# T chain on VectorE and ScalarE alone, last layer in two passes, attention steps in a written-out order

## Chip, cores and metric

One core of one Trainium2 chip. The metric is device time of one launch in microseconds (us). Engines in the text: TensorE (PE, with its weight loads PEld), VectorE (DVE), ScalarE (ACT), GpSimd (POOL) and SyncE (SP), which issues the DMAs.

## What is computed

Three layers in a row, on 3072 tokens (4 batches of 768) of width 384 (8 heads of 48). All of it is float32; `w_in` and `w_out` of the last layer arrive as float64 bits.

```python
# 1. linear attention with a complex decay, one state per head
mag = sqrt(a_re*a_re + a_im*a_im); scale = minimum(mag, 0.999) / (mag + 1e-6)
for t in range(768):                       # a = (a_re + i a_im) * scale
    S = a[t] * S + k[t] v[t]^T             # complex state 48 x 48, k and v real
    y[t] = q[t] @ real(S)
# 2. soft mixture of 8 experts with 4 slots each
logits = x @ phi
d = softmax over tokens; slot_input = d.T @ x
slot_out = relu(slot_input @ w1[e]) @ w2[e]
c = softmax over slots;  x = c @ slot_out
# 3. last layer, d_ff = 2048
h = maximum(x @ w_in, 0); out = (h * h) @ w_out
```

## The kernel before, in words

**Attention** works in 24 units of 128 tokens (6 per batch). The decay is taken in the log domain: for every chunk of up to three units (9 chunks, `TUS`), the **T chain** (`plan_t`, from L797) turns `a_re` and `a_im`, laid out as 128 x 3w with w = 128 to 384, into running sums of log magnitude (`t3`) and of angle (`t4`). Its steps in order: a clamp (L822, DVE), Ln and Exp (ACT), the ratio a_im / a_re by a multiply on GpSimd (L825), a clamp (L826, DVE), its square, Ln and a second square with a sum for a range flag (ACT), two combining steps (L830, L832, DVE) with an Exp between them, a running sum (three scans, L835, DVE), Arctan (ACT), again three scans, and a wrap into one turn (L842 to an integer, L845, DVE). `spans` and `waves` transpose the sums by unit (L881) and make from them E (exponentials) and W (cosine and sine).

Each unit (`plan_u`, from L935) multiplies q and k by E (`decay`, L964) and by W (`rotate`, L970) on DVE, transposes them on PE (`flip`, L988), copies them out of PSUM (`flop`, on ACT or DVE), makes four-head score blocks (`sc`, L1036), masks them on DVE (L1040), adds the unit's part to the state (`kv`, L1013; `keepS` keeps it), and forms y (`y1`, L1051 and L1056), which is copied (`ye`), transposed (`yb`, L1072) and copied again (`ya`). Every four units `grp_steps` adds to the token softmax; at the end `merge_steps` closes it.

**Order.** Every step is entered with `Plan.add` (engine, cost, due time, what it needs, buffers it takes and gives back). `Plan.issue` walks a modelled clock: whenever a modelled engine is free, it emits the ready step with the earliest due time, shifted by a table `SHIFT`. Where PE has nothing to do in the model, `warm` emits pairs of idle matmuls (L1169). The result is a fixed instruction stream per engine, executed in order on the chip. The 16 blocks of `w_in` are decoded from float64 among these steps (`plan_wi`, L1110; `f64_steps`: one ACT step and four DVE steps, L459 to L472). Weights of the experts are 16 loads of 1.5 MB (L491), three without a condition, six behind the end of the T chain and of the rotations (`l1` to `l3`), the rest when the attention's buffers are gone.

**After the steps** `grp_flags` (L493 to L503) makes the range flags on DVE and one matmul, the experts follow (`finish`: `up`, `turn`, `down`), and four of the 16 blocks of `w_out` are decoded beside them (`weights_out`).

**Last layer** (from L646): `seq` is 6 groups of 512 tokens by 16 blocks f of 128 hidden columns. Step n does on PE `up_last(n+2)` (one matmul, L680) and nine matmuls into three PSUM banks (`sh` times the high and the low part of w_out, `sl` times the high part, L729 and L726); ACT makes s and sh from the `up` result, DVE makes q (ACT for n = 1 to 11) and `sl` (GpSimd for n = 1 to 15, L697). In the first group each step also folds one `w_in` block with the experts' output (`make_G`, L668) and decodes one `w_out` block (`weights_out`). A group's three banks are copied out and stored after f = 15.

Of the kernel before, what the change touches and what calls it, by code (L numbers as in the profile page):

```python
# [11 lines left out]
F32 = mybir.dt.float32  # L12
# [12 lines left out]
NU = B * NCH  # L25
# [11 lines left out]
C_ID, C_CAUS, C_SEL, C_HM, C_BE, C_BO = 0, 128, 256, 544, 568, 600  # L37
C_W = 728
AR_MIN, AR_MAX, X_LIM, L_MIN = 1e-5, 1e18, 1.56, -65.0
R_MAX, X4_MAX, E_MIN = 2500.0, 5.9, 1e-26  # L40
# [3 lines left out]
SHIFT = {  # L44
# [3 lines left out]
    "across": -167.5, "back": -81.0, "bank": 277.5, "cos": -145.8, "decay": 8.4, "ends": 10.9, "exps": -7.8,  # L48
    "flip00": 13.5, "flip01": 17.2, "flip10": 8.4, "flip11": 1.7, "flop00": 0.5, "flop01": -7.4, "flop10": 0.4,
    "flop11": 9.4, "gather": 34.8, "keep": -203.0, "keepS": -7.6, "keep_c": 39.8, "keep_d": 387.9, "keep_l":  # L50
    -20.0, "keep_s": -201.7, "kv": -40.8, "l1": -34.8, "l2": 203.6, "l3": 305.6, "ld_a": -142.8, "ld_a1": 63.5,
    "ld_q": -102.8, "ld_raw": -133.3, "ld_v": 109.8, "less": 161.1, "logits": 12.6, "mask0": -50.2, "mask1": -1.2,
    "masked": -3.6, "over": -346.4, "pre": 127.7, "rot0": -69.6, "rot1": 7.7, "sc0": 9.7, "sc1": -8.7, "scale":
    -2.9, "share": 103.1, "size": 16.1, "slots": 137.4, "spread": 19.3, "sums": 331.4, "t3": -214.8, "t4": -274.4,
    "top": -22.5, "top_m": 39.4, "total": -24.9, "turn_d": -240.0, "turn_l": -54.1, "weight": -43.9, "wi0": -0.5,
    "wi1": 24.5, "wi2": 39.3, "wi3": -2.9, "wi4": 17.8, "y10": -57.3, "y11": 6.6, "y12": -65.0, "y13": -141.5,
    "ya": -1.5, "yb": 43.0, "ye": 5.7
}
WI_0, WI_P = 50.0, 10.909090909090908
# [7 lines left out]
def const_array():  # L67
# [12 lines left out]
    c[:, C_BO:C_BO + 128] = (p[:, None] % NS == p[None, :] % NS)  # L80
# [3 lines left out]
class Plan:  # L84
# [4 lines left out]

    LAG, LOAD, HOLD, KEEP, T_WARM, SECOND = 0.2, 1.28, 31.3, 0.43, 10.0, 325.2  # L90
# [4 lines left out]
    def add(self, eng, cost, due, fn, after=(), get=(), put=(), lat=0.0, tab=None, key=None):  # L95

        engs = [eng] if eng in ("PE", "SP") else list(eng)
        key = key or fn.__name__
        due += SHIFT.get(key, 0.0) + SHIFT.get(self.group, 0.0)
        self.steps.append((dict(zip(engs, cost if len(engs) > 1 else [cost])), due, fn,  # L100
                           [a for a in after if a is not None], get, put, lat, tab))
        return len(self.steps) - 1

    def issue(self, warm):
# [3 lines left out]
        ready = {"SP": [], "D": [], "A": [], "G": [], "PE": []}  # L108

        def enter(i):  # L110
            for e in self.steps[i][0]:
                ready[e].append(i)
        for i, s in enumerate(self.steps):
            for a in s[3]:
                users[a].append(i)
            if not missing[i]:
                enter(i)
        events, busy = [], {}
        now, done = 0.0, 0
        left = sum("PE" in s[0] for s in self.steps)  # L120

        def other(i):
            return self.steps[i][7] not in (None, self.loaded[0])

        def fits(i):
            get = self.steps[i][4]
            return all(self.free[g] >= get.count(g) for g in get)

        def due(i, eng):
            return self.steps[i][1] + self.HOLD * other(i) + self.SECOND * (eng == "D" and "A" in self.steps[i][0])  # L130
        while done < n:
            for eng, todo in ready.items():
                if busy.get(eng, 0) > now:
                    continue
                _, i = min(((due(i, eng), i) for i in todo if fits(i)), default=(0, None))
                if i is not None:
                    costs, _, fn, _, get, _, lat, _ = self.steps[i]
                    for e in costs:
                        ready[e].remove(i)
                    for g in get:  # L140
                        self.free[g] -= 1
                    left -= eng == "PE"
                    busy[eng] = end = now + costs[eng] + self.LOAD * other(i)
# [3 lines left out]
                elif eng == "PE" and left and events and now >= self.T_WARM and warm():  # L147
# [4 lines left out]
            while events and events[0][0] <= now + 1e-9:  # L152
                _, over, i = heapq.heappop(events)
                if over:
# [3 lines left out]
                    for j in users[i]:  # L158
                        missing[j] -= 1
                        if not missing[j]:  # L160
                            enter(j)
# [91 lines left out]
def moe_kernel(ctx, tc, raw, cst, aT, qk, vv_d, phi, w1, w2, w_in, w_out, out):  # L253
# [16 lines left out]
    lim = const.tile([128, 2], F32, name="lim")  # L270
# [22 lines left out]
    def grp_steps(g, st, p_s, ps_m):  # L293
# [64 lines left out]
        return [("PE", 1.18, logits, dict(needs="y", get=["pt"], put=["y"] * 4)),  # L358
                ("AD", (0.2, 0.25), keep_l, dict(put=["pt"])),
                ("D", 0.55, top, dict()),  # L360
                ("A", 0.5, exps, dict(tab=SET_EXP)),
                ("D", 0.1, total, dict(side=1)),
                ("PE", 0.11, turn_l, dict(get=["pt"])),
                ("AD", (0.16, 0.2), keep_c, dict(put=["pt"])),
                ("PE", 0.11, turn_d, dict(get=["pt"])),
                ("AD", (0.16, 0.2), keep_d, dict(put=["pt"])),
                ("PE", 0.75, sums, dict(needs="x", get=["pt"], put=["x"] * 4)),
# [880 lines left out]
```

## Time and profile before

| | |
|---|---|
| median of 3 runs | 576.48 us (575.58 to 578.71) |
| profiled execution | 572.69 us, of which the span is 570.9 us |
| PE busy in the span | 94% |
| DVE, ACT, POOL busy | 80%, 66%, 8% |
| attention: first to last instruction ahead of the experts | 0 to 288.35 us |
| experts | 288.35 to 316.42 us |
| last layer, until the last matmul | 316.42 to 564 us |

The profiled execution's own time is 3.8 us under the median. Busy shares are means over three stages with different limits, so the rows below are taken by stage. A row of a window gives the busy time of each engine in it; a row of a line gives count, busy time, mean of one, and the idle time in front with what ended it.

### The profile page before, as it was taken

Reading aid. Unit: us, or ns where it says so; the run is one execution under the profiler, and the core shown is the slowest. Engines: PE = TensorE matmul, PEld = TensorE weight load, DVE = VectorE, ACT = ScalarE, POOL = GpSimd, SP = SyncE. Lnnn points to the kernel's source line nnn. Section 1 sums busy time; section 2 is a strip of 40 time slices with the busy share of each in tenths; the row PEclk is TensorE's granted clock in tenths of the full one; section 3 lists DMA queues with packets and bytes.
Section 4 is the critical chain, followed back from the end, with each engine's and each line's share of the span. In section 5 each row is a group of like instructions: output and inputs, shape, how many; then the busy total and the mean of one; then the engine's idle time right before and its main releaser. Section 6 shows DMA issues by size and latency. Waiting matters only on the chain.

```text
span 570.9 us, 10386 instructions
## 1 busy us (share of the span) xinstructions
PE 534.1 (94%) x4080; PEld 430.2 (75%) x4080; DVE 454.4 (80%) x740; ACT 375.1 (66%) x684; POOL 45.2 (8%) x28
## 2 busy tenths in 40 slices
PE   1989999999998989999999997799999999999995
PEld 1977787878787878787843886588878888788884
DVE  3989999999999999998647799966666666666552
ACT  5887889888898868783213678555555555555551
POOL 1011020012001020000000133310000000000000
PEclk9999999999999989999999999799999999999999
DMA  8762342433415223398996133010010100100101
GB/s 304 295 259 87 111 124 85 151 115 111 125 44 171 67 65 116 122 386 311 396 389 254 55 112 103 10 56 1 0 57 0 57 0 0 56 2 0 56 1 61
DMA packets 23961, 67.25 MB, mean 118 GB/s; under 512 B 2144, under 2 KB 12256, under 8 KB 21856
## 3 DMA queue, kind: packets, MB, share of 16 engines
q1 hardware_dynamic: 23904, 66.51, 33.6%
q8 instruction: 34, 0.56, 0.4%
q14 instruction: 23, 0.19, 0.1%
HBM read 61.78 MB, written 4.72 MB: 116 GB/s over the span
## 4 chain that ended last, share of the span: by engine, by line
PE 61%; DVE 16%; ACT 1%; issue 1%; POOL 0%; DVEq 0%; POOLq 0%; ACTq 0%
PE po L729 20%; PE po L726 11%; PE pt L1036 4%; PE pt L988 4%; PE ph L680 3%; PE py L1051 3%; DVE t L835 2%; PE pt L527 2%; PE pS L1013 2%; PE py L1056 2%; DVE dw L472 2%; PE pt L1169 2%; DVE qke L964 1%; PE pt L542 1%; DVE dx L459 1%; DVE dx L469 1%
## 5 line engine op out<-in xcount | busy, mean ns | idle before, releaser
L729 PE MATMUL po<-sh,woh 128*128 128x512 f32 x288 | 114.5, 398 | 3.0 <-ACT sh L276 3.0
L729 PE MATMUL po<-sh,wol 128*128 128x512 f32 x288 | 114.2, 397 | 0.0
L276 ACT ACTIVATE s<-ph 128x512 f32<-128x512 f32 x96 | 57.2, 595 | 75.3 <-PE ph L680 72.9
L687 DVE TENSOR_TENSOR q<-s 128x512 f32<-128x512 f32 x85 | 60.6, 713 | 53.4 <-ACT s L276 53.3
L726 PE MATMUL po<-sl,woh 128*128 128x512 f32 x288 | 86.7, 403 | 1.2 <-POOL sl L697 1.2
L729 PEld LDWEIGHTS po<-sh,woh 128*128 128x128 f32 x288 | 54.6, 189 | 16.6 <-ACT sh L276 3.7
L726 PEld LDWEIGHTS po<-sl,woh 128*128 128x128 f32 x288 | 54.7, 192 | 16.0 <-POOL sl L697 3.3
L729 PEld LDWEIGHTS po<-sh,wol 128*128 128x128 f32 x288 | 54.6, 190 | 12.7
L697 DVE TENSOR_TENSOR sl<-q,sh 128x512 fp32r<-128x512 f32 x81 | 56.0, 692 | 9.6
L276 ACT ACTIVATE sh<-s 128x512 fp32r<-128x512 f32 x96 | 60.7, 633 | 3.5
L276 ACT ACTIVATE T<-pt 96x512 f32<-96x512 f32 x81 | 45.3, 593 | 17.9 <-PE pt L988 17.4
L1036 PE MATMUL pt<-T,T 96*128 96x128 f32 x384 | 52.0, 281 | 0.0
L1169 PE MATMUL pt<-cs 128*128 128x128 f32 x284 | 40.2, 291 | 12.0 <-DMA cs<-in_const_dram 11.8
L1036 PEld LDWEIGHTS pt<-T,T 96*128 96x128 f32 x384 | 46.2, 192 | 3.5 <-issue 3.0
L1169 PEld LDWEIGHTS pt<-cs 128*128 128x128 f32 x284 | 36.4, 202 | 14.2 <-DMA cs<-in_const_dram 11.8
L1051 PE MATMUL py<-am,v 128*48 128x128 f32 x384 | 40.9, 291 | 2.5 <-DVE am L1040 2.5
L680 PE MATMUL ph<-cT,G 128*128 128x512 f32 x96 | 39.8, 415 | 0.1
L825 POOL TENSOR_TENSOR a<-a,t 128x1152 f32<-128x1152 f32 (+2 forms) x9 | 24.3, 2702 | 180.6 <-ACT t L291 164.5
L835 DVE TENSOR_TENSOR_SCAN t<-a,lim 128x384 f32<-128x384 f32 (+2 forms) x39 | 36.7, 994 | 0.2 <-ACT a L291 0.2
L1040 DVE TENSOR_TENSOR am<-pt,cs 128x512 f32<-128x512 f32 x48 | 32.6, 682 | 4.3 <-PE pt L1036 3.7
L697 POOL TENSOR_TENSOR sl<-q,sh 128x512 fp32r<-128x512 f32 x15 | 20.7, 1384 | 147.6 <-PE ph L680 119.6
L1056 PE MATMUL py<-T,S 96*48 96x128 f32 x320 | 31.6, 275 | 0.0
(155 smaller groups left out, 931.9 us busy)
## 6 DMA issues: line engine op xcount, KB each, us to landing
w<-in_w_dram SPq DMA_DIRECT2D x16, 1536.0 KB, 9.3
qk<-in_qk_dram SPq DMA_DIRECT2D x24, 384.0 KB, 3.2
a<-in_a_dram SPq DMA_DIRECT2D x14, 576.0 KB, 4.2
raw<-in_wi_dram SPq DMA_DIRECT2D x16, 384.0 KB, 4.7
raw<-in_wo_dram SPq DMA_DIRECT2D x16, 384.0 KB, 3.1
v<-in_vn_dram SPq DMA_DIRECT2D x24, 192.0 KB, 2.4
out_dram<-o SPq DMA_DIRECT2D x18, 256.0 KB, 2.5
a<-in_a_dram SPq DMA_DIRECT2D x2, 384.0 KB, 6.1
```

The costliest lines, as they stand in the source:

```text
L276: return nc.scalar.activation(*args, **kw)
L680: mm(p, G[:, 128 * f:128 * (f + 1)], R["cT", g], start=True, stop=True)
L687: V.tensor_tensor(out=q, in0=s, in1=s, op=ALU.mult)
L697: (nc.gpsimd if 0 < n < 16 else V).tensor_tensor(out=sl, in0=s, in1=sh, op=ALU.subtract)
L726: mm(po[c], R["woh"][:, f, 128 * c:128 * (c + 1)], sl, start=False, stop=f == 15)
L729: mm(po[c], R[w][:, f, 128 * c:128 * (c + 1)], sh, start=f == 0 and w == "woh", stop=False)
L835: V.tensor_tensor_scan(out=v3(out)[:, j], data0=v3(src)[:, j], data1=low.to_broadcast([128, w]), initial=first[:, j:j + 1] if first is not ...
L1036: mm(p[:, C * h:C * (h + 1)], st["T", u, 1, g][:, h], st["T", u, 0, g][:, h], start=True, stop=True)
L1040: V.tensor_tensor(out=m, in0=st["pa", u, g].rearrange("p (h t) -> p h t", h=4), in1=cs[:, C_CAUS:C_CAUS + C].unsqueeze(1).to_broadcast([12 ...
L1051: mm(p[64 * w:64 * w + D, C * pr:C * (pr + 1)], st["v", u][:, h], st["am", u, h // 4][:, h % 4], start=True, stop=fst)
L1056: mm(p[64 * w:64 * w + D, C * pr:C * (pr + 1)], st["S", u][:, h], st["T", u, 0, h // 4][:, h % 4], start=False, stop=True)
L1169: mm(p[:, :C], ident, ident, start=True, stop=True)
```

## The change

1. **T chain.** Both clamps go (L822, L826), so does GpSimd: the ratio is a DVE multiply. The square and the flag's reduction are one DVE instruction (`tensor_tensor_reduce`, accumulating the maximum); both ACT squares go. The subtraction of L832 moves into the scan, whose second operand is now a full tensor in place of a broadcast limit; a one-operand minimum stays of L832. The conversion to an integer (L842) moves from DVE to ACT.
2. **Last layer.** `seq` goes through f = 0 to 7 for all six groups, then f = 8 to 15 for all six. Only 8 blocks of `w_in` are decoded in the attention; 8 of `w_in` and 8 of `w_out` are decoded beside the first pass, 2.4 pieces a step. The first pass copies its three banks to SBUF (two on ACT, one on DVE), the second adds them on DVE and stores. All `sl` and nearly all q are on DVE. PSUM: four banks for `up`, four for the sums.
3. **Order.** `SHIFT` and the due times no longer decide; `ORDER` lists all 1093 steps by engine, and `issue` takes each engine's list in that order. Costs in the plan are set anew.
4. Small: the merge's broadcast sum (`over`) is four matmuls of 32 rows.

In `ORDER`, the steps that may go on either engine are written into the list of one: 13 of the 96 `flop` copies, 3 `ye`, 4 `ya` and 2 first-unit `keepS` are in DVE's list. ACT's list changes its table 22 times. DVE's list ends with the last copy of the merge (`keep_s`), then two steps of the eighth `w_in` block, a memset and its last two steps.

```diff
-            step("D", D2, lambda: V.tensor_scalar(out=g("a0"), in0=g("a0"), scalar1=AR_MIN, scalar2=AR_MAX, op0=ALU.max, op1=ALU.min))
             step("A", A1, lambda: tact(SET_EXP, g("a0"), g("a0"), AF.Ln), tab=SET_EXP)
-            step("G", P1, lambda: nc.gpsimd.tensor_tensor(out=g("a1"), in0=g("a1"), in1=g("t2"), op=ALU.mult))
-            step("D", D2, lambda: V.tensor_scalar(out=g("a1"), in0=g("a1"), scalar1=X_LIM, scalar2=-X_LIM, op0=ALU.min, op1=ALU.max))
-            step("A", A1, lambda: act(g("t2"), g("a1"), AF.Square), key=("sq", v))
-            step("A", A1 + 0.09, lambda: act(g("t2"), g("t2"), AF.Square, accum_out=flags[:, 1, v:v + 1]), side=1, put=["t2"], key=("x4", v))
+            step("D", D1, lambda: V.tensor_tensor(out=g("a1"), in0=g("a1"), in1=g("t2"), op=ALU.mult), needs=("a1", v))
+            step("D", D1, lambda: V.tensor_tensor_reduce(
+                out=g("t2"), in0=g("a1"), in1=g("a1"), scale=1.0, scalar=0.0, op0=ALU.mult, op1=ALU.max,
+                accum_out=flags[:, 1, v:v + 1]), key=("sq", v))
-            step("D", D1, lambda: V.scalar_tensor_tensor(out=g("a0"), in0=g("a0"), scalar=LN_CLIP, in1=g("t3"), op0=ALU.min, op1=ALU.subtract))
+            step("D", D2, lambda: V.tensor_scalar(out=g("a0"), in0=g("a0"), scalar1=LN_CLIP, scalar2=None, op0=ALU.min))
-            step("D", D3, lambda: sums(g("t3"), g("a0"), ALU.max, lim[:, :1], None), put=["a0"], key=("L", v))
+            step("D", D3, lambda: sums(g("t3"), g("a0"), ALU.subtract, lambda j: v3(g("t3"))[:, j], None), put=["a0"], key=("L", v))
-            step("D", D2, lambda: V.tensor_scalar(out=g("a1").bitcast(I32), in0=g("t4"), scalar1=1.0 / (2 * math.pi), scalar2=None, op0=ALU.mult))
+            step("A", A1, lambda: act(g("a1").bitcast(I32), g("t4"), AF.Copy, scale=1.0 / (2 * math.pi)))
...
-                _, i = min(((due(i, eng), i) for i in todo if fits(i)), default=(0, None))
+                i = line[0]
+                if not missing[i] and all(self.free[g] >= get.count(g) for g in get):
+                    line.popleft()
...
-        for n in range(16):
+        for n in range(HALF):
             plan_wi(n)
...
+        jobs = [(1, f) for f in range(HALF)] + [(o, f) for f in range(HALF, 16) for o in (0, 1)]
...
+            seq = [(g, f) for fs in (range(HALF), range(HALF, 16)) for g in range(6) for f in fs]
+            def beside_last():
+                yield from pieces(R.pop("parts"))
+                for m in range(HALF, len(jobs), 2):
+                    yield from pieces(decode(m))
+                    steps = decode(m + 1)
+                    yield from pieces(steps[:3])
+                    make_G(jobs[m][1])
+                    yield from pieces(steps[3:])
+            rest, paced = beside_last(), [0]
...
-                if not 0 < n < 12:
+                if not 0 < n < 8:
                     V.tensor_tensor(out=q, in0=s, in1=s, op=ALU.mult)
-                (nc.gpsimd if 0 < n < 16 else V).tensor_tensor(out=sl, in0=s, in1=sh, op=ALU.subtract)
+                V.tensor_tensor(out=sl, in0=s, in1=sh, op=ALU.subtract)
...
+                if n < HALF:
+                    if f + 5 < HALF:
+                        make_G(f + 5)
+                    if f + 4 < HALF:
+                        weights_out(f + 4)
+                while paced[0] < (n - 3) * PACE and next(rest, True) is None:
+                    paced[0] += 1
...
+                        if f < HALF:
+                            o[g, c] = p_o.tile([128, 512], F32, name=f"o{g}{c}")
+                            copy("D" if c == 1 else "A", o[g, c], po[c])
+                        else:
+                            V.tensor_tensor(out=o[g, c], in0=po[c], in1=o[g, c], op=ALU.add)
+                            nc.sync.dma_start(out=out[128 * c:128 * (c + 1), 512 * g:512 * (g + 1)], in_=o[g, c])
```

## Rows read from the trace of the kernel before

**Rows 1.** The page: engine, busy us (share of span) and instructions; chain by engine.
```profile
PE 534.1 (94%) x4080; PEld 430.2 (75%) x4080; DVE 454.4 (80%) x740; ACT 375.1 (66%) x684; POOL 45.2 (8%) x28
PE 61%; DVE 16%; ACT 1%; issue 1%; POOL 0%; DVEq 0%; POOLq 0%; ACTq 0%
```

**Rows 2.** Windows: length, busy us of PE, PEld, DVE, ACT, POOL; clock, DMA share, GB/s.
```profile
0.00:288.35 288.35, 264.89 (x2644) 223.25 (x2647) 261.55 (x428) 222.19 (x407) 24.53 (x13) 0.99 0.51 174
...
40.00:250.00 210.00, 201.74 (x2056) 168.33 (x2056) 204.27 (x305) 178.04 (x329) 18.50 (x6) 0.99 0.38 120
250.00:278.00 28.00, 28.00 (x285) 22.33 (x285) 23.10 (x47) 12.44 (x25) 0.00 (x0) 1.00 0.93 354
...
316.42:376.20 59.78, 53.28 (x262) 43.09 (x263) 53.47 (x90) 42.02 (x90) 20.72 (x15) 0.94 0.22 65
376.20:564.00 187.80, 187.80 (x815) 151.51 (x813) 119.62 (x177) 101.84 (x168) 0.00 (x0) 1.00 0.06 22
```

**Rows 3.** PE groups from 39.19 (first scores) to 277.9: busy, mean ns, idle before.
```profile
L1051 PE MATMUL py<-am,v 128*48 128x128 f32 x384 | 40.9, 291 | 2.5 <-DVE am L1040 2.5
...
L881 PE MATMUL pt<-cs,t 128*128 128x128 f32 x126 | 18.9, 283 | 2.6 <-DVE t L835 2.6
...
L1169 PE MATMUL pt<-cs 128*128 128x128 f32 x85 | 13.4, 284 | 0.0
```

**Rows 4.** GpSimd's multiply, and DVE lines beside it: group, then min/median/max by line.
```profile
L825 POOL TENSOR_TENSOR a<-a,t 128x1152 f32<-128x1152 f32 (+2 forms) x9 | 24.3, 2702 | 180.6 <-ACT t L291 164.5
...
L964 DVE TENSOR_TENSOR qke<-qk,E 128x768 f32<-128x768 f32 x24 | 27.3, 1138 | 0.0
...
L964 DVE TENSOR_TENSOR qke<-qk,E x24: 933/949/2970, 26.9 to 256.1; 128x768 f32<-128x768 f32 x24
...
L903 DVE TENSOR_TENSOR ecr<-en,cs x9: 163/173/2593, 20.2 to 239.2; 128x24 f32<-128x24 f32 x9
...
L835 DVE TENSOR_TENSOR_SCAN t<-a,lim x30: 923/932/3323, 53.2 to 237.3; 128x384 f32<-128x384 f32 x30
```

**Rows 5.** Groups by shape: T chain and decode on DVE, from the start to 288.6.
```profile
L830 DVE SCALAR_TENSOR_TENSOR a<-t,a 128x1152 f32<-128x1152 f32 x7 | 9.4, 1348 | 0.0
...
L466 DVE SCALAR_TENSOR_TENSOR dx<-raw,dx 128x384 uint32<-128x384 uint32 x16 | 8.8, 549 | 0.1
...
L459 DVE TENSOR_SCALAR dx<-raw 128x384 uint32<-128x384 uint32 x16 | 5.6, 350 | 0.0
...
L842 DVE TENSOR_SCALAR a<-t 128x1152 int32<-128x1152 f32 x7 | 5.2, 749 | 0.0
```

**Rows 6.** Timeline of the first microseconds: start, length, engine, line [idle before].
```profile
8.92 0.99 POOL L825 TENSOR_TENSOR a<-a,t 128x384 f32<-128x384 f32 x1 [8.46 <-ACT t L291]
...
9.95 0.36 DVE L826 TENSOR_SCALAR a<-a 128x384 f32<-128x384 f32 x1 [2.49 <-POOL a L825]
...
27.80 4.23 DVE L835 TENSOR_TENSOR_SCAN t<-a,lim 128x256 f32<-128x256 f32 x3
```

**Rows 7.** Timeline where the experts begin.
```profile
287.56 0.26 DVE L419 COPY siT<-pt 128x96 f32<-128x96 f32 x1 [1.01 <-PE pt L416]
...
288.35 2.77 PE L527 MATMUL pt<-w,siT 128*4 128x256 f32 x46
```

**Rows 8.** Last layer: groups (L668 whole span, L472 316.42 to 376.2), timeline of PE.
```profile
L668 PE MATMUL ph<-wi,soT 128*128 128x128 f32 x96 | 12.9, 275 | 0.3 <-DVE soT L560 0.3
...
L472 DVE SCALAR_TENSOR_TENSOR dw<-dy,dx 128x384 f32<-128x384 f32 x12 | 11.0, 914 | 0.0
...
321.24 0.48 PE L680 MATMUL ph<-cT,G 128*128 128x512 f32 x1
...
363.20 0.50 PE L729 MATMUL po<-sh,woh 128*128 128x512 f32 x1 [2.29 <-ACT sh L276]
```

**Rows 9.** One step of the last layer as a window, columns as in rows 2.
```profile
367.39:371.54 4.15, 4.15 (x11) 3.13 (x10) 3.88 (x5) 2.75 (x5) 2.22 (x2) 0.52 0.00 0
```

More of the change, by code (lines that the diff above doesn't have):

```diff
@@ L1 @@
+from collections import deque
 from contextlib import ExitStack
@@ L35 @@
 SET_TRIG = 9
[L37 to L40, printed above, removed]
+C_ID, C_CAUS, C_SEL, C_HM, C_BE = 0, 128, 256, 544, 568
+C_W = 600
+R_MAX, X2_MAX, E_MIN = 2500.0, 2.43, 1e-26
 TB, EG = 8, 12
 NF = 3
-SHIFT = {
[3 rows of a table removed]
[L48 to L57, printed above, removed]
-}
-WI_0, WI_P = 50.0, 10.909090909090908
+ORDER = {
[6 rows of a table added]
+    ],
[16 rows of a table added]
+    ],
[18 rows of a table added]
+    ],
[20 rows of a table added]
+    ],
+}
+WI_0, WI_P = 150.0, 9.0
+HALF, PACE = 8, 2.4
 N_PRE, N_L, N_POST, N_GEN = 3, (2, 2, 2), 4, 7
@@ L115, in issue @@
                 users[a].append(i)
-            if not missing[i]:
-                enter(i)
-        events, busy = [], {}
+        todo = {e: deque(ORDER[e]) for e in ORDER}
+        assert sorted(sum(ORDER.values(), [])) == list(range(n))
+        events, busy = [(self.START, 0, -1)], dict.fromkeys(todo, self.START)
         now, done = 0.0, 0
[L120 to L130, printed above, removed]
         while done < n:
-            for eng, todo in ready.items():
-                if busy.get(eng, 0) > now:
+            for eng, line in todo.items():
+                if busy[eng] > now or not line:
                     continue
-                _, i = min(((due(i, eng), i) for i in todo if fits(i)), default=(0, None))
[L136 to L139, printed above, removed]
+                i = line[0]
+                costs, _, fn, _, get, _, lat, tab = self.steps[i]
+                if not missing[i] and all(self.free[g] >= get.count(g) for g in get):
+                    line.popleft()
                     for g in get:
                         self.free[g] -= 1
-                    left -= eng == "PE"
-                    busy[eng] = end = now + costs[eng] + self.LOAD * other(i)
+                    busy[eng] = end = now + costs[eng] + self.LOAD * (tab not in (None, self.loaded[0]))
                     fn(eng) if len(costs) > 1 else fn()
@@ L403, in over @@
         def over():
-            mm(bank()[:, :1], cs[:, C_BO:C_BO + 128], t["ws"], start=True, stop=True)
+            p = bank()
+            for j in range(4):
+                mm(p[32 * j:32 * j + 32, :1], cs[:, C_BE:C_BE + NS], t["ws"], start=True, stop=True)
         def scale():
@@ L572, in enter @@
             R["c4"] = pool("p_c4", 1, **side)
[L573 to L574 removed]
+            R["c"] = pool("p_c", 1, **side)
+            load_job(2)
             used(2)
[L577 to L585 removed]
@@ L587, in part, with load_job @@
-        def part(n):
-            sl = slice(n, n + 1)
-            act(R["woh"][:, sl], R["dw", n], AF.Copy)
-            V.tensor_tensor(out=R["wol"][:, sl], in0=R["dw", n], in1=R["woh"][:, sl], op=ALU.subtract)
+        jobs = [(1, f) for f in range(HALF)] + [(o, f) for f in range(HALF, 16) for o in (0, 1)]
+        def load_job(n):
+            if n < len(jobs):
+                o, f = jobs[n]
+                p = p_raw if n % 3 < 2 else R["more"]
+                R["raw", n] = t = p.tile([128, 1, DM, 2] if o else [128, 3, 128, 2], U32, name="raw")
+                nc.sync.dma_start(out=t, in_=w_out[f // 2][:, f % 2:f % 2 + 1] if o else w_in[f])
@@ L593, in weights_out, with pieces @@
+        def pieces(steps):
+            for fn in steps:
+                fn()
+                yield
         def weights_out(n):
-            steps = decode(n) if n < 16 else []
-            for fn in steps[:4]:
-                fn()
-            if 0 < n < 17:
-                part(n - 1)
-            for fn in steps[4:]:
-                fn()
-            load_wo(n + 3)
+            steps = decode(n)
+            for fn in steps[:4] + R.pop("parts", []) + steps[4:6]:
+                fn()
+            R["parts"] = steps[6:]
@@ L950, in plan_u @@
             t0 = at(u)
+            plan.group = f"u{u}"
             def lq():
```

138 lines of the change are left out of this document (63 added, 75 removed), and 63 rows, old and new, of tables (ORDER, SHIFT).

## The prediction

> **What bounds the kernel now.** I read the page first: PE is busy 94% of the span, and the chain that ends last is 61% PE and 16% DVE [rows 1]. A mean over three stages decides nothing, so I cut the span into windows [rows 2]. Three things are to be seen there. From 40 to 250 us DVE is busy 204.27 of 210 us: the middle of the attention is paced by DVE. PE is busy 201.74 of the same 210, but not all of that is work: from the first scores at 39.19 to 277.9, 13.4 us are idle matmuls of L1169, and 2.5 and 2.6 us of open waits for DVE stand in front of y and of the transposes [rows 3]. So PE has 18.5 us of slack in a stretch of 238.7, and that, not DVE's load, is the most that a lighter DVE can give back there. From 250 to 278 PE has no gap while DVE has 4.9 us of them [rows 2]. The experts change in nothing but a small merge step. In the last layer the first 16 steps run from 321.24 to 376.20, 54.96 us, with DVE busy 53.47 of 59.78; the other 80 take 187.80, 2.35 each, PE without a gap and DVE at 64% [rows 2, 8].
>
> **GpSimd goes.** Its nine multiplies are busy 24.3 us, and DVE instructions beside them stretch: L964 has a median of 949 ns, a mean of 1138 and a longest of 2970; L903, 173 ns long, reached 2593; a scan of 932 reached 3323 [rows 4]. L964 alone loses 24 x 0.189 = 4.5 us, the longest of the other two 2.4 us each, and the scans at 27.80 took 4.23 us for three, where 932 ns for a larger one would make it 2.8 at most: at least 10.7 us together [rows 4, 6]. The upper end is all of GpSimd's 24.3. I take 13, near the lower end, because that one is counted line by line.
>
> **T chain on DVE.** In units of a full chunk (1152 wide; the nine chunks make eight of them): out go two clamps and the integer conversion at 0.75 each and a combining step at 1.35, in come a minimum at 0.75, the ratio and the fused square at 1.35 each, by the rows of L842 and L830 [rows 5]. 3.60 out, 3.45 in: 8 x 0.15 = 1.2 us gained. The scan with a full second operand is priced as the scan, 932 ns for 384 [rows 4]. No row shows the fused square with its accumulated maximum. Its lower end is the plain two-operand row, 1.35; its upper end is the slowest two-operand row per element, the scan: three of 0.93, 2.8 us, which would add 8 x 1.45 = 11.6 us. I take 1.35: the row of the same shape.
>
> [...] No run of the kernel before has an accumulating DVE instruction of two sources; L830 and L964, without one, show about 1.2 ns per element. [...]
>
> **Eight decodes move.** Four DVE steps, 0.35 and three of 0.55: 2.0 us a block, 16 us for eight [rows 5]. Each also takes one ACT step and one DMA on SP out of the attention; ACT has 32 us free between 40 and 250 [rows 2], and takes the integer conversion (one step a chunk) for the two squares that go. DVE then has 261.55 - 13 - 1.2 - 16 = 231 us to do [rows 2]; the few copies that change engine by the written list are within 2 us.
>
> **What it gives in the attention.** DVE drops by 30, but PE is next: 18.5 us of slack. Between 250 and 278 PE already runs gapless, so the schedule can be dense when DVE isn't short. I take 15 of the 18.5 and leave 3.5 for waits that a lighter DVE doesn't end (ends: 5 and 18.5). At the start the ratio takes 0.99 us on GpSimd at 8.92 and a clamp of 0.36 follows it, and the scans at 27.80 lose at least 1.4 [rows 6]; over three early chunks, with the hand-overs between engines, I take 4 us off the 39.19 (ends 0 and 10: DVE still has three chunks to push through before it is level). Against it: the written list puts two decode steps, a memset and two more decode steps behind the merge's last copy on DVE. At 287.56 that copy is followed by the flags, whose matmul stands in front of the experts on PE at 288.35 [rows 7]. The flags now wait for 0.35 + 3 x 0.55 and the memset: 2 us later, with the whole PE queue of the experts behind. Attention: 15 + 4 - 2 = 17 us.
>
> **Loads.** SP issues the last four conditional weight loads behind the last three `w_in` loads and the last v loads, as now behind such loads; the DMA share of 250 to 278 is 0.93 [rows 2], so this queue has little room, but three fewer `w_in` blocks fall into it. I cost it at nothing; each 1.5 MB load that came late and uncovered would cost 4.4 us, by its 1536 KB over the 354 GB/s of that stretch.
>
> **Last layer.** PE's work is 96 steps at 187.80 / 80 = 2.35, and 11 `make_G` blocks at 12.9 / 16 = 0.81 [rows 2, 8]: 225.4 + 8.9 = 234.3, against 54.96 + 187.80 = 242.8 now. Its lower bound is thus 8.5 us better, if nothing stalls. DVE: 119.62 / 80 = 1.50 a step in the clean part; 2.4 pieces a step, 14 pieces being two decodes (4.0 us), a low part (0.55) and a G half (0.35): 0.84; group work twice as often, an allowance of 0.15. That is 2.49 a step for steps 4 to 50, against PE's 2.35 + 0.81 x 2.4 / 14 = 2.49. Level, with in-order hand-overs in it: an ACT step of a decode waits for the DVE step in front, and the next `s` queues behind it on ACT. `L472` shows what is saved: 914 ns beside GpSimd for 547 to 549 without [rows 5, 8]. The cover for the decodes is DVE's free 36%; it is used up, not exceeded. I take 2.5 us of stalls (ends 0 and 12). Six us remain. The 18 added evacuations of the first pass lie beside PE (banks rotate), the adds of the second pass are 18 x 0.7 on a DVE that is then free.
>
> **Sum.** 17 + 6 = 23 us off 572.7, the profiled execution: 549.7. Its own time is 3.8 under the median shown, so the forecast for the median is 553.5.
>
> **Rivals.**
> (a) *PE isn't the next limit* and DVE alone sets the end of the attention. For: DVE is the one that is full from 40 to 250. Against: PE without a gap from 250 to 278, with DVE at 83% [rows 2]. Then 288.35 - 30 + 2 = 260, attention gains 28, all 34: 542.5. [...] Weight loads are 80% from 40 to 250; but they are 80% from 250 to 278 too (22.33 of 28), where PE never waits, so here 80% looks like full.
> (b) *The fused square runs like the scan*: 11.6 us more on DVE, which brings it to 243, as near to its limit as PE; about 5 us of the gain go: 558.5.
> (c) *Hand-overs bind the last layer*: DVE and ACT wait on each other in steps 4 to 50, 0.2 us a step: 47 x 0.2 = 9 us on top: 562.5. For: both are level by the sum above.
> (d) *The written order fits the modelled clock and not the chip*: PE's queue then stands behind a step that is late while others are ready. That happens now too (5.1 us, rows 3); if the slack stays and only the start and the last layer gain: 568.
> [...]
> That the change doesn't take effect (the range flags send the launch through the fallback) is excluded by the data: the squared ratio stays far under 2.43 with a_re at 0.85 or more and a_im of a tenth.
>
> **How the numbers follow.** Forecast 0.50; (a) 0.17; (b) 0.12; (c) 0.12; (d) 0.05; (e) 0.04. The predicted time is the forecast's, 553.5. The range takes in (a) to (c) with their spread: 541 to 566. Faster by over 0.5% (about what a measurement of this kernel can tell from no change) are all but (e), the late side of (d) and a little of (c): 0.93; within 0.5% 0.03; slower 0.04.
>
> **What would show it.** First experts' matmul at about 271 instead of 288.35, with a gap of about 2.5 us behind the merge; L1169 between first scores and last y at some 4 us instead of 13.4; no DVE instruction of three times its median; the fused square at 1.35 (2.7 shows (b)); DVE over 95% busy in steps 4 to 50 with PE gaps of 2 to 3 us in all, clock 1.00. Wrong if the attention ends before 265 (a) or after 280 (d), or if the last layer takes over 250 us from its first G to its last matmul (c, e).

## The result, and the profile of the changed kernel

The changed kernel takes 551.62 us (median of 4 runs, 550.95 to 552.83), the kernel before beside it 576.67 (575.58 to 578.71, 4 runs): ratio 0.9564, 95% interval 0.9532 to 0.9596. The forecast was 553.5. The profiled execution spans 550.1 us against 570.9, so 20.8 us are to be found in the two traces. The medians are 25 us apart; the other 4 are not in the traces, since the profiled execution of the kernel before is 4.0 us under its median here and the changed kernel's 0.3 over.

The page of the changed kernel, engines and chain, answers [rows 1]:

```profile
PE 520.2 (95%) x4006; PEld 417.1 (76%) x4006; DVE 447.4 (81%) x774; ACT 361.9 (66%) x664; POOL 0.2 (0%) x4
...
PE 86%; DVE 9%; ACT 1%; DMA 1%; issue 1%; SPq 1%; DVEq 0%; ACTq 0%
```

The chain went from 61% PE to 86%. To see where, I cut every trace at the same five instructions on PE: first scores, last `yb` (the last matmul of the attention chunks), first matmul of the experts, first `make_G`, and the last matmul with the low part of `w_out` (three with `sl` follow it). All are starts, from the view of one line's instructions. "Tail" is the merge and the flags. The lengths add up to the span; all runs told of below stand in the same table.

| kernel (profiled execution) | start | attention | tail | experts | last layer | end | span |
|---|---|---|---|---|---|---|---|
| before | 39.2 | 238.5 | 10.6 | 28.1 | 247.4 | 7.1 | 570.9 |
| changed | 36.8 | 217.3 | 13.3 | 29.7 | 245.0 | 8.0 | 550.1 |
| e1 flags early | 37.3 | 217.3 | 10.4 | 29.9 | 244.2 | 7.0 | 546.1 |
| e2 cT early | 35.9 | 217.4 | 13.3 | 31.2 | 242.0 | 7.0 | 546.8 |
| e3 both | 36.0 | 217.4 | 10.4 | 30.2 | 242.7 | 6.5 | 543.2 |
| e4 multiply on GpSimd | 38.3 | 220.4 | 13.3 | 30.8 | 245.7 | 7.7 | 556.2 |
| e7 new chain, old order | 32.3 | 249.4 | 10.6 | 28.1 | 246.9 | 7.8 | 575.1 |
| e8 chain and two passes, old order | 32.3 | 250.7 | 10.6 | 28.1 | 245.1 | 7.6 | 574.4 |
| e9 more VectorE work | 37.8 | 222.9 | 13.3 | 29.5 | 243.7 | 6.9 | 554.1 |
| e10 more PE work | 35.5 | 227.4 | 13.3 | 30.7 | 245.3 | 8.2 | 560.4 |
| e11 old work, fitted order | 41.8 | 232.7 | 11.0 | 28.1 | 247.0 | 6.9 | 567.5 |
| e12 new chain, fitted order | 35.0 | 218.6 | 10.8 | 30.6 | 247.0 | 7.8 | 549.8 |
| e13 all of it, other fitted order | 34.6 | 220.6 | 10.1 | 28.1 | 244.0 | 6.6 | 544.0 |
| e14 e3, order refitted | 36.4 | 223.2 | 9.8 | 28.4 | 242.6 | 7.5 | 547.9 |

Of the 20.8 us, 2.4 come from the start, 21.2 from the attention and 2.4 from the last layer; the tail gives back 2.7, the experts 1.6, the end 0.9.

Windows of the changed kernel, columns as in [rows 2]: the attention, the experts, then the last layer's steps 0 to 47, its steps 48 to 95, and 2.6 us inside the first of these.

```profile
36.80:254.40 217.60, 217.60 (x2260) 178.56 (x2259) 199.39 (x314) 173.71 (x326) 0.00 (x0) 1.00 0.45 156
...
267.40:297.10 29.70, 29.39 (x365) 12.69 (x365) 19.03 (x45) 8.56 (x19) 0.00 (x0) 0.95 0.86 340
```

```profile
302.40:422.60 120.20, 113.98 (x519) 91.83 (x518) 108.10 (x198) 80.09 (x151) 0.00 (x0) 0.99 0.19 57
422.60:543.60 121.00, 120.16 (x520) 97.03 (x518) 84.54 (x130) 64.32 (x107) 0.00 (x0) 1.00 0.10 35
322.40:325.00 2.60, 2.60 (x6) 2.06 (x7) 2.46 (x5) 1.68 (x3) 0.00 (x0) 0.50 0.27 28
```

In the attention PE has no gap at all, and VectorE, with 227 us of work before [rows 2], has 199. Of the idle matmuls, 13.4 us in [rows 3], 3.2 are left. The groups of that stretch and of the T chain (columns as in [rows 3] and [rows 5]):

```profile
L1228 PE MATMUL pt<-cs 128*128 128x128 f32 x20 | 3.2, 280 | 0.0
```

```profile
L1023 DVE TENSOR_TENSOR qke<-qk,E 128x768 f32<-128x768 f32 x24 | 22.7, 945 | 0.0
...
L883 DVE CUSTOM_DVE_ANT_0 t<-a 128x1152 f32<-128x1152 f32 x7 | 9.4, 1348 | 0.0
L887 DVE SCALAR_TENSOR_TENSOR a<-t,a 128x1152 f32<-128x1152 f32 x7 | 9.4, 1348 | 0.0
```

`qke` has a mean of 945 ns where [rows 4] had 1138, and its longest is 958 where it was 2970; the longest scan takes 1014 ns, the longest `ecr` 183 (3323 and 2593 there). None of these lines is stretched any more. L883 is the fused square with its maximum, at 1348 ns; reading its accumulator (a row of its own) adds a median of 82 ns.

All waits of PE in the last layer (what waited <- what ended the wait: us in total, times, the longest; `cT` are the transposed mixture weights of a group of tokens, made from `c`), and the start of the experts in the timeline (start, length, engine, line, [idle before]):

```profile
PE ph L730 <- DVE cT L653: 4.4, 3, 2.5
PE ph L648 <- DVE c L643: 1.8, 1, 1.8
PE ph L707 <- DVE soT L590: 0.3, 1, 0.3
```

```profile
264.21 0.26 DVE L449 COPY siT<-pt 128x96 f32<-128x96 f32 x1 [0.71 <-PE pt L446]
264.39 0.35 DVE L489 TENSOR_SCALAR dx<-raw 128x384 uint32<-128x384 uint32 x1
264.77 0.56 DVE L496 SCALAR_TENSOR_TENSOR dx<-raw,dx 128x384 uint32<-128x384 uint32 x1
265.41 0.38 DVE L1217 MEMSET pt<- 128x384 f32 x1
265.70 0.54 DVE L499 SCALAR_TENSOR_TENSOR dx<-raw,dx 128x384 uint32<-128x384 uint32 x1
266.27 0.56 DVE L502 SCALAR_TENSOR_TENSOR wi<-dy,dx 128x384 f32<-128x384 f32 x1
...
267.43 0.16 PE L532 MATMUL pt<-all_ok 128*1 128x1 f32 x1 [3.25 <-DVE all_ok L530]
...
267.46 4.30 PE L557 MATMUL pt<-w,siT 128*4 128x256 f32 x46
```

The decode behind the merge delays the flags as forecast (3.25 us of PE idle). What follows was not forecast: after that gap the first 46 matmuls of the experts take 4.30 us where [rows 7] has 2.77, the clock of this stretch being 0.64 (the row stands in the last section).

### The profile page after: what moved, and what is told of

Read it like the earlier page. It is cut to its first block, busy times and chain, and to the rows that moved or that the text cites. A ratio compares the mean times of both kernels' runs of the same rounds, so it can differ in the third digit from the quotient of the medians.

```text
span 550.1 us, 10120 instructions
## 1 busy us (share of the span) xinstructions
PE 520.2 (95%) x4006; PEld 417.1 (76%) x4006; DVE 447.4 (81%) x774; ACT 361.9 (66%) x664; POOL 0.2 (0%) x4
## 4 chain that ended last, share of the span: by engine, by line
PE 86%; DVE 9%; ACT 1%; DMA 1%; issue 1%; SPq 1%; DVEq 0%; ACTq 0%
PE po L784 21%; PE po L781 10%; PE pt L1047 9%; PE pt L1095 8%; PE py L1110 6%; PE pS L1072 5%; PE pt L1228 5%; PE ph L730 4%; PE pt L939 3%; PE py L1115 3%; PE pt L557 2%; PE pt L1131 2%; DVE sl L747 2%; PE pt L572 1%; PE pt L334 1%; DMA a<-in_a_dram 1%
## 5 line engine op out<-in xcount | busy, mean ns | idle before, releaser
L747 DVE TENSOR_TENSOR sl<-q,sh 128x512 fp32r<-128x512 f32 x96 | 66.3, 691 | 10.9 <-ACT q L304 1.3
L304 ACT ACTIVATE T<-pt 96x512 f32<-96x512 f32 x83 | 47.4, 593 | 11.0 <-PE pt L1047 10.5
L939 PE MATMUL pt<-cs,t 128*128 128x128 f32 x144 | 23.6, 282 | 12.7 <-DVE t L893 12.7
L1072 PEld LDWEIGHTS pS<-v,KN 128*96 128x96 f32 x320 | 29.4, 165 | 2.0 <-issue 2.0
L314 ACT ACT_TABLE_LOAD x23 | 29.5, 1283 | 1.1 <-PEq L1298 0.7
L1072 PE MATMUL pS<-v,KN 128*96 128x48 f32 x320 | 30.0, 247 | 0.0
L1047 PE MATMUL pt<-cs,KN 128*96 128x128 f32 x192 | 29.9, 278 | 0.0
```

The costliest lines, as they stand in the source:

```text
L304: return nc.scalar.activation(*args, **kw)
L747: V.tensor_tensor(out=sl, in0=s, in1=sh, op=ALU.subtract)
L939: tr(pe[:, C * j:C * (j + 1)], x[:, j, C * i:C * (i + 1)], ident)
L1047: tr(pt[:96, C * h:C * (h + 1)], X[:, 4 * g + h].rearrange("p c d -> p (c d)"), ident)
L1072: mm(pS[:96, D * h:D * (h + 1)], st["KN", u][:, h].rearrange("p c d -> p (c d)"), st["v", u][:, h], start=not seeded, stop=not seeded or h ...
```

## The experiments

The theory to test was the prediction's: VectorE paced the attention; a lighter VectorE hands the limit to PE; the order only has to be no worse than before. Rivals: VectorE is still the limit; or the gain is the order's.

**Is PE now the limit, and how far off is VectorE?** e10 makes the first of the four transposing steps of a chunk do its work twice (96 matmuls more, same result); e9 runs the fused square twice.

```
e10:  for h in [0, 1, 2, 3] * (2 if s == g == 0 else 1):   # flip00
e9:   lambda: [V.tensor_tensor_reduce(... same operands ...) for _ in range(2)]
```

> The first four transposes of every unit are done twice: 96 more matmuls of PE, 24 x 0.44 to 0.53 = 10.5 to 12.7 us of PE work in the attention and nothing else. Theory (PE sets the pace): 9 to 13 us more, 560.5 to 564.5. Rival (DVE is the limit, PE has room): under 4 us more, under 555.5.

Measured: 562.23 (559.28 to 563.23), ratio 0.9738 (0.9672 to 0.9804). The added matmuls are 10.5 us of PE time (this line's group went from 29.7 to 40.2) and the attention is 10.1 longer: each is paid in full, as the theory has it. PE is the limit, with the weight loads at 188.71 of 227.70 us, 83%.

> The fused square of the T chain is done twice: nine more DVE instructions, about 10 us of DVE work in the attention and nothing else. Theory (PE sets the attention's pace now, DVE has some 11 us free between 40 and 228): under 4 us more, 552 to 555.5. Rival (DVE is still the limit): the whole 10 us, 561.

Measured: 560.67 (555.84 to 562.70), ratio 0.9734 (0.9673 to 0.9796). The median is that of the rival. But the four runs differ: 555.84 at a mean granted clock of 0.993, which was profiled, and 559.94 to 562.70 at 0.983 to 0.986, so that in the median the added work and a lower clock come together. In the profiled execution VectorE has 207.04 us to do in 223.20, 7.7 more than in the changed kernel, and the attention is 5.6 longer, the span 4.0. The waits of PE from first scores to last `yb`:

```profile
PE pt L939 <- DVE ec L974: 1.8, 1, 1.8
PE pt L1047 <- DVE QN L1029: 1.1, 1, 1.1
PE py L1110 <- DVE am L1099: 0.8, 2, 0.6
PE pt L1047 <- DVE KN L1029: 0.4, 1, 0.4
```

So neither theory is right alone. PE is the limit, but the 18 us in which VectorE is idle are not 18 us of slack: in an order that is fixed, most of what is added to it arrives at PE (5.6 of 7.7 us in this trace).

**What GpSimd cost.** e4 puts one line back.

```
- lambda: V.tensor_tensor(out=g("a1"), in0=g("a1"), in1=g("t2"), op=ALU.mult)
+ lambda: nc.gpsimd.tensor_tensor(out=g("a1"), in0=g("a1"), in1=g("t2"), op=ALU.mult)
```

> The changed kernel with one line put back: the ratio multiply on GpSimd. VectorE loses 8 full chunks x 1.35 = 10.8 us of work and gets back whatever GpSimd's 24 us beside it cost. Theory of the prediction (contention of about 13 us): VectorE ends 2 us heavier and has some 7 us of slack against PE, so 551.5 to 554.5, with the scans and qke beside the multiply stretched again (a mean of L1023 above 1.1 us). Rival 1 (GpSimd costs all of its 24.3 us): VectorE 13.5 us heavier, as in the run with two fused squares: 559 to 562. Rival 2 (contention is under 5 us): 549 to 551.5.

Measured: 560.57 (557.73 to 563.64), ratio 0.974 (0.9693 to 0.9788). The time is rival 1's, its reason isn't. VectorE, groups of the attention, e4:

```profile
L1023 DVE TENSOR_TENSOR qke<-qk,E 128x768 f32<-128x768 f32 x22 | 24.1, 1096 | 1.0 <-DMA qk<-in_qk_dram 0.9
...
L887 DVE SCALAR_TENSOR_TENSOR a<-t,a 128x1152 f32<-128x1152 f32 x6 | 10.1, 1678 | 0.0
...
L883 DVE CUSTOM_DVE_ANT_0 t<-a 128x1152 f32<-128x1152 f32 x6 | 8.1, 1351 | 3.6 <-POOL a L882 3.6
```

The multiply that left VectorE was 8.1 us of the attention. VectorE's busy time there fell by 1.4 (199.12 to 197.74 us), so the stretching took back 6.7, beside 19.5 us of GpSimd: 3.3 on `qke` (20.8 to 24.1), 2.0 on L887, the rest smaller. The prediction's size for the contention (13 for 24.3 us of GpSimd) was of the right order. But e4 is slower with a VectorE that is no busier: by 9 us in the median, by 6 to 7 in its two runs at the changed kernel's clock (0.989 and 0.990; the other two are at 0.980 and 0.981). In its profile the start is 1.5 longer and the attention 3.1; another 1.1 lie in the experts, where the clock behind the flags' gap was 0.50 for longer (0.88 in the mean from 250 to 278 us, where the changed kernel has 0.94). The multiply takes 2.77 us instead of 1.35, and VectorE stands 3.6 us behind it at L883. A delay inside the chain costs time though no work is added; how much of it is the longer multiply and how much the stretched instructions, this run does not separate.

**The chain without the order.** e7 is the kernel before with the new T chain only; e8 has the two-pass last layer and the moved decodes as well. Both keep the due times, step prices and other settings of the planner of before, the hand-set shifts mapped to the steps that are left.

```
e7:  plan_t from the changed kernel; SHIFT keys T0..T15 mapped to its 13 steps
e8:  e7, and finish() from the changed kernel; plan_wi for HALF blocks
```

> The kernel before with the new T chain alone (no GpSimd in it, no clamps, squares off ScalarE), its order still found by due times, its last layer as it was. Theory of the prediction (the lighter chain gives VectorE 14 us and the start 4, and PE is not yet the limit): 576.6 - 18 = 558.6, within 556 to 562; idle matmuls fall from 13.4 us to about 5. Rival (the due times, tuned for the old chain, leave the steps in a poor order, and the gain needs the written-out order): 566 to 575, with PE waits on T's scans of over 5 us.

> The kernel before with the new T chain and the last layer in two passes with half of the decodes beside it: everything of the change but the written-out order. If the order is worth nothing by itself: 550.5 to 553.5, as the changed kernel. If the order is what fills PE: 556 to 566, with idle matmuls and waits on VectorE of over 6 us between first scores and last y, where the changed kernel has 3.15 and none. The last layer should take 245 us from its first G to its last matmul in either case.

Measured: e7 576.53 (575.84 to 577.73), ratio 1.0002 (0.9980 to 1.0025); e8 580.35 (576.18 to 580.67), ratio 1.0060 (1.0034 to 1.0086). Neither theory holds, and e8 lies above its second branch (556 to 566) too. This is the result that decides the case: the whole removal of work, in the old way of ordering, is worth nothing. (The profiled execution of e8 is its shortest, 576.18 at a mean clock of 0.995; most of its runs are at 0.986 to 0.987 and 580.4, so that what it is slower than e7 goes with the clock.) The attention of e7 as a window, and its idle matmuls (L1168 there, the line that is L1228 in the changed kernel):

```profile
32.30:281.90 249.60, 242.19 (x2444) 201.72 (x2444) 224.02 (x363) 188.50 (x345) 0.00 (x0) 1.00 0.44 147
```

```profile
L1168 PE MATMUL pt<-cs 128*128 128x128 f32 x185 | 28.7, 284 | 0.0
```

The start is 6.9 us shorter, as a lighter chain promises. Then the attention is 10.9 longer, with 28.7 us of idle matmuls instead of 13.4, VectorE idle for 25.6 of 249.6 us and PE waiting besides. No engine is full. The wait rows are small and scattered (1.5 us for T's scans where e7's rival wanted over 5): the idle matmuls fill the gaps that the planner itself leaves. e8 shows the same with VectorE at 213.77 of 251.00, and in its last layer, 245.1, it is 1.8 shorter than e7 (246.9).

**The order without the chain, and both.** For e11 to e13 I wrote out an order for each kernel's own steps: starting from what its due times gave, single steps were moved in the queues as long as the planner's clock, with the step prices of the changed kernel, ended earlier; the same effort for each. e11 is all the work of before, e12 is e7's, e13 is the changed kernel's.

```
- SHIFT = {...}; ready lists sorted by due time
+ ORDER = {"SP": [...], "D": [...], "A": [...], "G": [...], "PE": [...]}; Plan of the changed kernel
```

> The kernel before with all of its work (GpSimd's multiply, the clamps, sixteen decodes, the last layer in one pass), but its attention steps issued in a written-out order that was fitted to this work, with the step prices of the changed kernel. Theory (VectorE, busy 228 of the 238.7 us from first scores to last y, is the limit of the old work, and an order can take away only its gaps): 8 to 11 us less, 565 to 569. Rival (the order is the whole gain in the attention, and the removed work is worth nothing by itself): 555 to 559, with idle matmuls under 6 us and no waits of PE between first scores and last y. Other rival (the contention with GpSimd, which no price of a step has in it, spoils a fitted order): 572 to 577.

> The kernel before with the new T chain and a written-out order fitted to that work by the same effort; sixteen decodes and the last layer in one pass stay. Theory (order and a lighter chain together; VectorE then has 224 us to do, PE 217): 554 to 558, the attention from first scores to last y in 220 to 226 us. Rival (VectorE has to lose the eight decodes as well before PE can run without a gap): 560 to 566.

> The changed kernel with its written-out order replaced by another one, fitted to the same steps from the order that the due times gave (the one of the run at 580). Theory (any order fitted to the new work lets PE run without a gap): within 3 us of the changed kernel's 551.6. Rival (the change's own order holds something that this one doesn't): 556 or more.

Measured: e11 569.92 (568.21 to 576.99), ratio 0.9920 (0.9882 to 0.9957); e12 551.52 (550.34 to 555.88), ratio 0.9591 (0.9524 to 0.9657); e13 546.66 (545.87 to 548.20), ratio 0.9498 (0.9439 to 0.9556). The attention as a window, e11 and then e12, and e11's longest waits of PE in it:

```profile
41.80:274.80 233.00, 221.81 (x2253) 181.04 (x2254) 212.13 (x332) 188.96 (x355) 20.39 (x6) 0.99 0.47 162
```

```profile
35.00:253.90 218.90, 218.66 (x2270) 180.45 (x2274) 206.07 (x335) 182.26 (x344) 0.00 (x0) 1.00 0.48 164
```

```profile
PE py L1079 <- DVE am L1068: 3.4, 2, 2.2
PE pt L1016 <- DVE QN L998: 2.2, 2, 1.4
PE pt L1016 <- DVE KN L998: 2.1, 1, 2.1
PE pt L1064 <- ACT T L304: 1.5, 2, 0.9
```

Put side by side: the order alone gives 0.8%, the chain alone 0.0%, both together 4.1%. That is no sum; each is worth its gain only beside the other. With the old work, PE in a fitted order still waits for VectorE (8 us in e11, idle matmuls 2.5); with the new chain and its order it waits 0.4 us in all. The theory for e11 held but for the size (569.9, expected 565 to 569), e12 did better than its theory (551.5, expected 554 to 558), and e13, expected within 3 us of 551.6, was 5 us faster: its attention is 3.3 us longer than the changed kernel's, with 0.7 us of gaps of PE, and what it gains lies at the start (2.2), at the flags (3.2), where the eighth decode doesn't delay them, in the experts (1.6) and in the last layer (1.0). Two things stay open here. The fit for e11 knew nothing of the contention with GpSimd, so another order might give the old work more than 0.8%. And due times refitted to the new chain, in place of a written-out order, were not tried.

e12 says one thing more. It keeps all sixteen decodes ahead of the last layer and the single pass, and its attention takes 218.6 us, where the changed kernel takes 217.3: the eight decodes did not have to leave. e13, with the move, is 5.8 us shorter in span than e12, but 3.0 of that lie in the last layer and 2.5 in the experts; its attention is 2.0 longer. In medians the intervals of e12 and e13 overlap, so of the second part of the change only the last layer's 2 to 3 us are shown, and the clock is in them: in e12's last layer it fell to 0.50 for some 3 us, in e13's not at all (the longest matmul with `sh` takes 0.63 and 0.50 us, the mean clock of the two executions is 0.994 and 0.999).

**Two repairs.** e1 issues the flags' VectorE steps inside the merge; e2 makes the transposed coefficients `cT` two steps earlier, and those of group 1 ahead of step 0; e3 is both; e14 is e3 with the order refitted from the changed kernel's own, as above.

```
e1:  share():  + if not rows_done: flag_rows()      # compare, reduce, memset
     grp_flags():  only the matmul and the copy are left
e2:  - if f == 3 and n < 5 * HALF: spread_c(g + 1)
     - if f == 5 and n < 5 * HALF: make_cT(g + 1, wide)
     + if f == 1 and HALF <= n < 5 * HALF: spread_c(g + 1)
     + if f == 3 and HALF <= n < 5 * HALF: make_cT(g + 1, wide)
     + spread_c(1) in the expert layers, make_cT(1, wide) behind make_G(4)
```

> The five DVE steps of the range flags are issued inside the merge (behind `share`), ahead of the last copy, and no longer behind the eighth w_in decode. Theory: PE's gap ahead of the experts, 3.25 us in the changed kernel, falls to about 0.5, and the 46 first expert matmuls, 4.30 us there at a lowered clock, take 2.8: 3.5 to 4.5 us less, 547.6. Rival one (the clock falls for the merge's idle matmuls, whatever the gap): 2.5 us less, 549. Rival two (PE really waits for the expert weights or for siT): no change, 551.6.

Measured: 548.53 (547.46 to 549.38), ratio 0.9515 (0.9456 to 0.9573). The tail is 10.4 us again, the wait for the flags is gone, and the clock in the experts is 1.00. The time lies between the theory (547.6) and rival one (549), but the clock speaks for the theory: the merge has the same 56 idle matmuls as in the changed kernel, and it did not fall. What is missing to the theory is in the experts, which still take 29.9 us. In e3, where it is the same, the rows read:

```profile
281.06 0.37 ACT L307 ACTIVATE hs<-pt 128x256 f32<-128x256 f32 x1
...
285.90 0.55 ACT L307 ACTIVATE dy<-raw 128x384 f32<-128x384 f32 x1 [4.47 <-DMA raw<-in_wo_dram]
286.35 0.51 ACT L307 ACTIVATE woh<-dw 128x384 fp32r<-128x384 f32 x1
286.77 0.37 ACT L307 ACTIVATE hs<-pt 128x256 f32<-128x256 f32 x1
...
287.19 0.44 PE L572 MATMUL pt<-cs,hs 128*128 128x128 f32 x2 [1.28 <-ACT hs L307]
```

The experts now begin at 264 instead of 288, a `w_out` block has not landed yet, and ScalarE waits 4.47 us in its decode with `hs`, the copy of the first expert product that PE transposes next, queued behind it. PE loses 2 us to it in two waits. In e13, whose experts begin at 265.3 and take 28.1, no such wait is seen; it issues two 1.5 MB blocks of expert weights fewer after 225 us. So the attention has become short enough to meet the loads; moving these was not tried.

> The combination weights of the next group (cT) are made earlier: those of group 1 before the first step of the last layer, the others at f = 3 in place of f = 5 (their spread at f = 1 in place of 3). Theory: cT is simply ready too late, PE waits for it four times (1.8, 2.5, 0.5, 1.5 us) and once runs 1.4 us longer at a lowered clock: 5 to 7.5 us less, 545.5. Rival (DVE and ACT are full in steps 0 to 10 and in pass one at large, so the same work ahead of time delays something else): the waits move in front of the sl matmuls, under 2 us gained, 550 to 552.

Measured: 549.69 (548.60 to 549.90), ratio 0.9533 (0.9477 to 0.9590). The last layer takes 242.0 us instead of 245.0, and no wait for `cT` is left. That is half of what the theory forecast (545.5), and in the median the rival's "under 2 us": new waits of 2.4 us stand in front of the output matmuls (for `sh`, `sl` and a copy of the sums). 1.5 us of the gain are lost in the experts of that execution (31.2), where the clock was 0.91 behind the flags' gap.

> The changed kernel with both repairs at once: the flags' vector steps issued inside the merge, and the transposed coefficients of a group made before they are wanted. Theory (the two stalls lie on the path one behind the other, each with its own microseconds): the savings add up, 3.1 for the flags (551.62 to 548.53) and 1.9 for the coefficients (551.62 to 549.69): 546.6, within 545.5 to 547.5. Rival (the second saving is only a different roll of the clock, which fell in the expert layers of the profile with the early coefficients): no more than the flags alone, 548 to 549.

Measured: 546.14 (544.53 to 547.79, 6 runs), ratio 0.9481 (0.9451 to 0.9511). The two add up: the theory's 546.6. The rival, 548 to 549, does not fit: though the intervals of e1 and e3 overlap, the last layer is 1.5 us shorter than e1's and has no wait for `cT`, and the clock stayed at 1.00 in both. It is faster than the changed kernel: the two intervals are apart.

> Both repairs (flags inside the merge, early coefficients), and the written-out order refitted from the changed kernel's own. Between first scores and last y PE has nothing to give but 3 us of idle matmuls, so what another order can still save lies before the first scores (36 us; 32.3 in the two runs with due times): theory 541 to 545. Rival (PE's work is the limit from the first microseconds on, what starts earlier waits later): 545.5 to 547.5 as with both repairs alone.

Measured: 548.53 (546.51 to 549.63, 6 runs), ratio 0.9512 (0.9466 to 0.9558): no gain, and above the rival's range too. The planner's clock promised one; on the chip PE stands still once, for a load that the planner takes to be in time, and behind that the clock is 0.50 from 223.5 to 230.3 us (mean of this execution 0.991, of e3's 0.999):

```profile
PE pS L1072 <- DMA v<-in_vn_dram: 3.7, 1, 3.7
```

## Why the prediction was right, and where it was not

The total was 1.9 us off. The terms were further off and partly cancelled. So did the last step: for a profiled execution the forecast was 549.7, and 551.92 was measured, 2.2 too few; the 3.8 us added to get from a profiled execution to the median did not come (the changed kernel's is 0.3 over its median), which turned 2.2 too few into 1.9 too many. That the sum is so near is in part luck.

**VectorE's relief: right.** Forecast 30 us less, measured 227.4 between 40 and 278 us [rows 2] against 199.12 between 36.8 and 254.1: 28. The fused square came at the price taken, 1.35 us, so rival (b) falls. The trace has 1348 ns for it, the same as L887 without an accumulator, and 82 ns for the read of it. Rival (b) priced the harm at 5 us; e9, whose second square adds about as much work, measures 4 in the profiled execution and 9 in the median, where the clock is lower too.

**PE next: right; its slack: too small.** Forecast 15 of 18.5, measured 21.2. The prediction added 13.4 us of idle matmuls and the two longest waits; with the small rows (1.5, 1.0, 0.5) the waits were 8.1, so the slack was 21.5. It also left 3.5 for waits that a lighter VectorE doesn't end; only 3.2 us of idle matmuls stayed. The remaining 2.9 us are PE's other work, which is that much shorter in the new trace. Two things in the traces are behind it. In the kernel before, the clock fell to 0.50 from 208 to 211 us, behind a wait of 1.71 us for the masked scores (`am`); half of that stretch, 1.5 us, is an estimate of what it cost. And 16 matmuls of `kv` (L1072, 1.5 us) and 6 of the transposed sums (L939, 1.0 us) come ahead of the first scores in the changed kernel and behind them before. Rival (a) falls: e10 pays every matmul in full (10.5 us added, the attention 10.1 longer), at 83% weight load. The sixth of the stretch in which no weights were loaded was no headroom; this agrees with the prediction's reading of [rows 2], 80% of weight load both where PE waits and where it never does.

**The step that failed: the order was costed at nothing.** The prediction has VectorE's relief turn into PE's time by itself and treats the written order only as a risk, rival (d) at 0.05. The runs show that the gain does not come without it: e7 and e8, everything but the order, are at 1.000 and 1.006 of the time before. What they show is a misfit of order and work as in rival (d), larger than that was priced (576 to 580 instead of 568), only that it is the old due times that misfit; the written order itself fitted the chip, with no gap of PE in the attention. The forecast came out right because the change brings the order with it. I could have seen the risk in the code: the due times carry some ninety shifts, one for each kind of step, and the change removes or moves some of the steps that they belong to. How far e7's loss is that of those shifts, and how far that of my mapping of them, stays open; e12 shows that the order is what is missing.

**Eight decodes: right in size, wrong in worth.** 16 us left VectorE, and the prediction counted them into the relief. e12 keeps them, and PE runs just as full.

**GpSimd: right in size.** In the trace of before the lines stretched in the attention sum to 11 us: `qke` 22 x 0.21 = 4.6, KN 23 x 0.08 = 1.9, scans 30 x 0.08 = 2.4, `ecr` 7 x 0.34 = 2.4, each its mean against the undisturbed one. With the start, 13 was a fair value. e4 adds that time is lost even where VectorE's load does not rise.

**Start: 4 forecast, 2.4 measured.** The chain could do more: e7, e8 reach the first scores at 32.3 us. e13 suggests that this alone is not worth much: its first scores come 2.2 us earlier than the changed kernel's, and its attention is 3.3 longer. That what starts earlier meets the same full PE is the likely reason; no run tests it alone.

**Tail: 2 forecast, 2.7 measured, and a follow-up missed.** The mechanism was the one described; e1 takes it away. The 1.6 us behind it, the clock in the experts (0.64 over the first 4.5 us), were not foreseen, though [rows 9] shows the same thing in the last layer (0.52).

**Last layer: 6 forecast, 2.4 measured.** PE's own work came out as forecast: 113.98 and 120.16 us in the two halves against 234.3. The mis-sized term is the stalls, 2.5 in the prediction. PE lost 6.5 us to waits, 4.4 of them for `cT`, and in the window from 322.40 ran at 0.50, matmuls 0.63 us long, where those ahead of the wait took 0.40. VectorE was not level with PE in that pass but 90% busy (108.10 of 120.20), where the prediction had over 95%: it is one hand-over that came late, not the load. The prediction counted the group work "twice as often", 0.15 us a step, and not when it is due: with eight steps a group instead of sixteen, `cT` is made at step 5 and wanted at step 6, two ahead of its use. With that mended, e2 gains 5.4 us on before. Rival (c), VectorE and ScalarE waiting on each other at every step, did not happen. Rival (e), at 0.04, has the kernel slower than before through a lower clock in the first pass: it was lower there for one stretch of about 2.6 us from 322.40 (0.50), and the mean of the pass is 0.99.

## What to carry to other kernels

Work taken off the busiest engine and the order of what is left are one change: priced apart, neither gave more than 0.8% here, together 4.1% (e11, e7, e12). When a planner's priorities are fitted to a set of steps, refit them before judging a change of the steps, or the judgement is that of the misfit. And when a loop is cut in half, look at each hand-over's distance in steps, not only at its work.

## What the runs showed of the hardware beyond expectation

An engine's idle share was not slack: VectorE, idle 18 of 217.6 us, turned 7.7 us of added work into 5.6 us of time (e9), and nine steps moved to GpSimd, up to 1.4 us longer each there, made start and attention 4.6 us longer with VectorE no busier (e4).

Behind some single gaps of PE the granted clock was lower: in the changed kernel 3.25 us of idle, then 46 matmuls in 4.30 us instead of 2.77, window clock 0.64 from 267.4 to 271.9; the same gap in e2 and e10 (3.3 us) was followed by 0.50 for 4.0 and 4.8 us. Without the gap (e1, e3, e12, e13) the clock in the experts stayed at 1.00. But the length of a gap does not tell whether the clock falls: behind the wait of 2.47 us for `cT` it was 0.50 in the changed kernel, and behind the same wait of 2.47 and 2.48 us 1.00 in e13 and e1 (longest matmul with `sh` 0.50 and 0.45 us, 0.63 in the changed kernel); behind the wait of 1.71 us that ended at 206 us in the kernel before it fell to 0.50.

```profile
267.40:271.90 4.50, 4.47 (x52) 1.83 (x52) 0.14 (x1) 0.43 (x2) 0.00 (x0) 0.64 1.01 426
```
